# Attention denominators without the tensor engine: four one-column matmuls replaced, in 90 of 128 units, by a transposing VectorE sum and five GpSimd instructions

## The chip, the cores and the metric

The kernel runs on one core of a Trainium2 chip. Five engines with instruction queues of their own take part: TensorE (PE in the profile, its weight loads listed as PEld), VectorE (DVE), ScalarE (ACT), GpSimd (POOL) and SyncE (SP), which here only starts transfers. Engines meet through semaphores. The metric is the device time of one execution in microseconds (us); lower is better.

## The reference

The input `A_x` (2048 rows of 512) is normalised per row. Two branches start from the result `xn`, and their product is added to the input:

```
xn = layernorm(x)
s  = attention(xn, k_cache, v_cache, wq, wo)   # 32 heads of 128, 2048 queries, 2048 keys
g  = silu(mixer_mlp(xn, w1, w2, w3, w4))
return x + s * g
```

In the attention, `q = xn @ wq`, `p = softmax(q k^T / sqrt(128))`, `o = p v` for each head, and the heads' outputs are multiplied by `wo` and added. The softmax needs, for every query and head, the sum of 2048 exponentials; `o` is divided by it. Matrices are bfloat16; the scores need no maximum subtracted, since the inputs are small.

## The kernel before

The start (to about 147 us) computes layernorm, the mixer and most of the MLP. The attention follows and takes nearly all of the rest. It is cut into 128 units: 8 groups of 4 heads, in each group 4 blocks of 512 queries, in each block the 4 heads (`units`, head innermost). A unit is computed with keys on the partitions and queries along the free axis, in 8 slots (`SPU`), so that the main loop counts slots `n`, and `u, p = divmod(n, 8)`.

In slot p of unit u these things are issued, in this order:

- `s_slot(u, p)`: two matmuls of 128 keys by 512 queries into one PSUM tile `ps_s` (two buffers), and ScalarE's `exp` of it into a quarter of `pT` (L283).
- `pv_slot`, five slots behind: two matmuls that add `v` times those exponentials to `ps_o` (two buffers, each held from slot 5 of its unit until `norm` has read it).
- in slots 0 and 1 `q_mm(u + 1)`, two matmuls each, that make the next unit's queries in the one PSUM buffer tagged `xa`; in slot 2 VectorE's `q_copy` (L267) empties it.
- in slot 0 `add_last(u - 1)`: the exponentials of a unit are added up on VectorE over the 16 key blocks, with `add_first` (L289, slot 4), `add_next` (L294, slot 6 and slot 0 of the next unit) and two halving adds (L299, L300). What is left is `acc[:, 0, :]`: 128 partitions (keys) by 512 queries, still to be summed over the partitions.
- in slot 2 `norm(u - 2)` (L333): VectorE multiplies `ps_o` by the reciprocal denominators `rb` and writes `oT`.
- in slot 3 `sums(u - 1)` (L311 to L321): four matmuls with a quarter of `acc` each as the weights (every fourth query) and a column of ones as the moving side sum over the partitions, into 128x4 numbers in PSUM (also tag `xa`). VectorE's `reciprocal` (L319) reads them, and SP stores the result `rc` to a small DRAM tile `dr` (L321).
- in slot 4 `bcast(u - 1)` (L325): SP reads `dr` back, copied to all 128 partitions, as `rb`, 128 by 512 floats.
- in slots 4 to 6 `wo_mm` and `wo_post` for one finished 128-row tile of a block: four matmuls, and VectorE's add into `sacc` (L365).

All instructions are kept in the order of the program on their engine (`pin`). SP's queue therefore holds, per unit, the store of `rc`, the load of `rb` behind it, and behind these, in slots 5 to 7, the loads of the next group's keys (`load_k`, L132), values (`load_v`, L142) and weights. The keys of a group's last head are loaded in slots 5 and 7 of two successive units just ahead of the unit that uses them.

GpSimd's queue holds small layernorm work at the start (`rsqrt`, L167 an add and L168 a power, on 128x1 numbers) and the loads of `x` for the last group's outputs (`fin_load`, L355, emitted from unit 117 on); in the units between it has nothing.

Of the kernel before, what the change touches and what calls it, by code (L numbers as in the profile page):

```python
# [9 lines left out]
ALU = mybir.AluOpType  # L10
FP32 = mybir.dt.float32
# [6 lines left out]
def kernel(  # L18
# [15 lines left out]
    nc = tc.nc  # L34
    P = nc.NUM_PARTITIONS
# [15 lines left out]
    HG = 4  # L51
# [10 lines left out]
    pin = tc.keep_in_program_order  # L62

    def pool(name, bufs=1, space=None, **kw):
        if space is not None:
            kw["space"] = space
        return tc.tile_pool(name=name, bufs=bufs, **kw)

    ent = ctx.enter_context
    const = ent(pool("const"))  # L70
    xnT = const.tile([P, DC, Sq], BF16, name="xnT")
    xall = const.tile([P, NT, D], BF16, name="xall")
    ones_t = const.tile([P, 1], BF16, name="ones_t")
    nhalf = const.tile([P, 1], FP32, name="nhalf")
    mv1 = const.tile([P, NT, nc.vector.BN_AGGR_DIM], FP32, name="mv1")
    mv2 = const.tile([P, NT, nc.vector.BN_AGGR_DIM], FP32, name="mv2")
    rs1 = const.tile([P, NT], FP32, name="rs1")
# [9 lines left out]
    smp = ent(pool("smp", 4))  # L87
    tokp = ent(pool("tok", 4))
    drp = ent(pool("drp", 4, bass.MemoryType.DRAM))
# [15 lines left out]
    def mm(out, lhsT, rhs, start, stop):  # L105
        pin(nc.tensor.matmul(out=out, lhsT=lhsT, rhs=rhs, start=start, stop=stop))  # L106

    pin(nc.vector.memset(warm[:], 0.0))
    pin(nc.vector.memset(ones_t[:], 1.0))
    pin(nc.vector.memset(nhalf[:], -0.5))  # L110
    pin(nc.gpsimd.iota(diag[:], pattern=[[-1, P]], base=0, channel_multiplier=1,
                       allow_small_or_imprecise_dtypes=True))
    pin(nc.vector.tensor_scalar(
        out=ident[:], in0=diag[:], scalar1=0.0, scalar2=None, op0=ALU.is_equal))

    units = [(g, qt, hh) for g in range(NG) for qt in range(QT) for hh in range(HG)]
    NU = len(units)
    NS = NU * SPU
    kTs, vBs, wqs, wos, oTs, st = {}, {}, {}, {}, {}, {}
# [136 lines left out]
    def q_mm(u, dcs, tag="xa"):  # L256
        g, qt, hh = units[u]
        if dcs[0] == 0:
            st[u] = dict(psq=psX.tile([P, 512], FP32, tag=tag, name="ps_q"))
        for dc in dcs:  # L260
            mm(st[u]["psq"][:], wqs[g * HG + hh][:, dc, :],
               xnT[:, dc, qt * 512:(qt + 1) * 512], dc == 0, dc == DC - 1)

    def q_copy(u, eng=None):
        qT = qtp.tile([P, 512], BF16, name="qT")
        if eng is None:
            pin(nc.vector.tensor_copy(out=qT[:], in_=st[u].pop("psq")[:]))  # L267
        else:
            pin(nc.scalar.activation(out=qT[:], in_=st[u].pop("psq")[:], func=ACT.Identity))
        st[u]["qT"] = qT  # L270

    def s_slot(u, p):
        g, qt, hh = units[u]
        s = st[u]
        sps = psS.tile([P, 2, 512], FP32, name="ps_s")
        for j in range(2):
            kc = 2 * p + j
            kv = kTs[g * HG + hh].rearrange("d (i p j) -> d i j p", p=P, j=KJ)
            mm(sps[:, j, :], kv[:, kc // KJ, kc % KJ, :], s["qT"][:], True, True)
        if p % 2 == 0:  # L280
            s.setdefault("pT", []).append(pB.tile([P, 4, 512], BF16, tag="pT", bufs=4, name="pT"))
        jj = 2 * (p % 2)
        pin(nc.scalar.activation(  # L283
            out=s["pT"][-1][:, jj:jj + 2, :], in_=sps[:], func=ACT.Exp, scale=SCALE))
# [7 lines left out]
    def add_next(u, i):  # L292
        a = st[u]["acc"]
        pin(nc.vector.tensor_tensor(out=a[:], in0=a[:], in1=st[u]["pT"][i][:], op=ALU.add))  # L294

    def add_last(u):
        add_next(u, 3)
        a = st[u]["acc"]
        pin(nc.vector.tensor_tensor(out=a[:, 0:2, :], in0=a[:, 0:2, :], in1=a[:, 2:4, :], op=ALU.add))  # L299
        pin(nc.vector.tensor_tensor(out=a[:, 0, :], in0=a[:, 0, :], in1=a[:, 1, :], op=ALU.add))  # L300

    def pv_slot(u, p):
        g, qt, hh = units[u]
        s = st[u]
        if p == 0:
            s["o"] = psO.tile([P, 512], FP32, tag="ps_o", name="ps_o")
        pT = s["pT"][p // 2]
        for j in range(2):
            kc = 2 * p + j
            mm(s["o"][:], vBs[g * HG + hh][:, kc, :], pT[:, 2 * (p % 2) + j, :], kc == 0, kc == KC - 1)  # L310

    def sums(u):
        s = st[u]
        ps = psX.tile([P, 4], FP32, tag="xa", name="ps_sum")
        a = s["acc"][:, 0, :].rearrange("k (p j) -> k j p", j=4)
        for j in range(4):
            mm(ps[:, j:j + 1], a[:, j, :], ones_t[:], True, True)
        rc = smp.tile([P, 4], FP32, name="rc")
        pin(nc.vector.reciprocal(out=rc[:], in_=ps[:]))  # L319
        s["dr"] = drp.tile([P, 4], FP32, name="dr")  # L320
        pin(nc.sync.dma_start(out=s["dr"][:], in_=rc[:]))  # L321

    def bcast(u):
        st[u]["rb"] = pB.tile([P, 512], FP32, tag="rb", bufs=2, name="rb")
        pin(nc.sync.dma_start(  # L325
            out=st[u]["rb"][:], in_=st[u]["dr"][:].rearrange("p j -> (p j)").partition_broadcast(P)))

    def norm(u):
        g, qt, hh = units[u]
        s = st.pop(u)  # L330
        if hh == 0:
            oTs[(g, qt)] = pB.tile([P, HG, 512], BF16, tag="oT", bufs=2, name="oT")
        pin(nc.vector.tensor_tensor(  # L333
            out=oTs[(g, qt)][:, hh, :], in0=s["o"][:], in1=s["rb"][:], op=ALU.mult))
# [8 lines left out]
    def wo_mm(g, t, hhs, ps=None):  # L343
        if hhs[0] == 0:
            wo_box[0] = psX.tile([P, D], FP32, tag="xm", name="ps_wo") if ps is None else ps
        oT = oTs[(g, t // 4)]
        ts = t % 4
        for hh in hhs:
            mm(wo_box[0][:], oT[:, hh, ts * P:(ts + 1) * P], wos[g * HG + hh][:], hh == 0, hh == HG - 1)
# [3 lines left out]
    def fin_load(t):  # L353
        xl = tokp.tile([P, D], BF16, tag="ta", bufs=10, name="xl")
        pin(nc.gpsimd.dma_start(out=xl[:], in_=xsrc[t]))  # L355
        fin[t] = xl

    def wo_post(g, t):
        ps = wo_box.pop(0)
        if g == 0:  # L360
            sacc[t] = pS.tile([P, D], FP32, tag="sacc", bufs=NT, name="sacc")
            pin(nc.vector.tensor_copy(out=sacc[t][:], in_=ps[:]))
            return
        sa = sacc[t][:]
        pin(nc.vector.tensor_tensor(out=sa, in0=ps[:], in1=sa, op=ALU.add))  # L365
        if g < NG - 1:
            return
        xl, gl = fin.pop(t), xall[:, t, :]
        pin(nc.vector.scalar_tensor_tensor(  # L369
            out=gl, in0=sa, scalar=0.5, in1=gl, op0=ALU.mult, op1=ALU.mult))  # L370
        pin(nc.vector.tensor_tensor(out=xl[:], in0=gl, in1=xl[:], op=ALU.add))  # L371
        pin(nc.sync.dma_start(out=out2d[t * P:(t + 1) * P, :], in_=xl[:]))
# [158 lines left out]
            at(n + 4, lambda: gate_silu(t, th["a"]))  # L531

    wo_todo = deque()
    for n in range(NS + 3 * SPU):
        u, p = divmod(n, SPU)
        if u < NU:
            g, qt, hh = units[u]
            s_slot(u, p)
        m = n - LAG
        if 0 <= m < NS:  # L540
            pv_slot(*divmod(m, SPU))
        if p in (0, 1) and 4 * HG - 1 <= u < NU - 1:
            q_mm(u + 1, (2 * p, 2 * p + 1))
        if p == 0 and 1 <= u <= NU:
            add_last(u - 1)
        if p == 2 and 4 * HG - 1 <= u < NU - 1:
            q_copy(u + 1)
        if p == 2 and 2 <= u <= NU + 1:
            norm(u - 2)
            if units[u - 2][2] == HG - 1:  # L550
                gg, qq = units[u - 2][:2]
                wo_todo.extend((gg, 4 * qq + ts) for ts in range(4))
                if gg == NG - 1:
                    fin_load(4 * qq)
        if p == 3 and 1 <= u <= NU:
            sums(u - 1)
        if p == 4 and 1 <= u <= NU:
            bcast(u - 1)
        if p in (4, 5) and wo_todo:
            wo_mm(*wo_todo[0], (0, 1) if p == 4 else (2, 3))  # L560
        if p == 6 and wo_todo:
            gg, t = wo_todo.popleft()
            wo_post(gg, t)
            if gg == NG - 1 and t % 4 < 3:
                fin_load(t + 1)
        if p == 4 and u < NU:
            add_first(u)
        if p == 6 and u < NU:
            add_next(u, 2)
        held_mm(n)  # L570
        for fn in todo.pop(n, ()):
            fn()
        if not held and not todo.get(n + 1) and pS is None and n >= 4 * SPU + 5:
            right.close()
            pS = right.enter_context(pool("pS", side="right", reuse_waits="tile"))
# [38 lines left out]
```

## Time and profile before

| what | value |
|---|---|
| median of 3 runs | 1289.25 us (1289.19 to 1290.49) |
| the profiled execution | 1289.44 us, its span 1287.6 us, so 1.84 us lie around the span |
| granted TensorE clock, mean | 0.991 |
| PE busy | 1257.4 us, 98% of the span |
| ACT busy | 1054.8 us, 82% |
| DVE busy | 942.5 us, 73% |
| POOL busy | 47.5 us, 4%, nearly all of it before 76 us and after 1175 us |
| `norm` of unit to `norm` of unit, 330 to 1110 us | 89 of them from 334.8 to 1106.5: 8.77 us each |

The span is the time from the first to the last instruction. A group line gives busy time, then the mean duration of one, then how long its engine sat idle just before and who ended that. Overlapping matmuls are drawn longer than they keep the engine from the next, so distances between starts tell more than durations.

### The profile page before, as it was taken

What the parts mean: (1) busy time and instruction counts of PE and PEld (TensorE: products, weight loads), DVE (VectorE), ACT (ScalarE), POOL (GpSimd) and SP (SyncE); (2) the same over time, 40 slices, a digit from 0 to 9 for tenths busy, and PEclk for the clock granted to TensorE, in tenths of its full rate; (3) what the DMA queues carried; (4) which work ended last, traced back from release to release, by engine and by line L of the source; (5) the groups of instructions that cost most, each with busy time, mean ns of one, the idle gap of its engine ahead of it and who ended that gap; (6) DMA issues with size and microseconds to landing.
All of it is one profiled execution on the core that took longest, in us unless ns stands there. A gap on an engine that the chain in (4) does not pass through costs nothing.

```text
span 1287.6 us, 16764 instructions
## 1 busy us (share of the span) xinstructions
PE 1257.4 (98%) x6128; PEld 609.6 (47%) x6252; DVE 942.5 (73%) x1316; ACT 1054.8 (82%) x1101; POOL 47.5 (4%) x115
## 2 busy tenths in 40 slices
PE   7999999999999999999999999999999999999995
PEld 3444444444444444444444444444444444444442
DVE  6721467777777777777777777777777777778886
ACT  4344779998888888888888888888888888888882
POOL 5320000000000000000000000000000000000000
PEclk9999999999999999999999999999999999999997
DMA  9293122443144522452145423451244323442211
GB/s 209 45 172 74 21 46 50 82 91 67 41 74 77 97 34 51 90 96 46 48 83 77 79 42 59 90 95 33 55 91 78 62 51 72 85 82 43 65 43 49
DMA packets 170771, 91.57 MB, mean 71 GB/s; under 512 B 124928, under 2 KB 153088, under 8 KB 170688
## 3 DMA queue, kind: packets, MB, share of 16 engines
q1 hardware_dynamic: 166464, 84.72, 34.3%
q0 software_dynamic: 1824, 4.98, 1.7%
q8 instruction: 49, 0.80, 0.3%
q10 hardware_dynamic: 2400, 0.79, 0.2%
q14 instruction: 34, 0.28, 0.1%
HBM read 67.63 MB, written 2.36 MB: 54 GB/s over the span
## 4 chain that ended last, share of the span: by engine, by line
PE 89%; DVE 6%; DMA 2%; ACT 1%; issue 1%; POOL 0%; another core or an unknown queue 0%; SPq 0%; DVEq 0%; ACTq 0%
PE ps_s L106 36%; PE ps_o L106 35%; PE ps_wo L106 8%; PE ps_q L106 7%; DVE acc L294 2%; PE ps_m L106 2%; PE ps_sum L106 1%; ACT pT L283 1%; DVE sacc L365 1%; DVE xall L369 1%; DVE acc L299 1%; DMA kT<-in_A_k_cache_dram 1%; DVE qT L267 0%; DVE xl L371 0%; DMA xnT<-xall 0%
## 5 line engine op out<-in xcount | busy, mean ns | idle before, releaser
L283 ACT ACTIVATE pT<-ps_s 128x1024 bf16<-128x1024 f32 x1024 | 993.1, 1026 | 135.3 <-PE ps_s L106 130.4
L106 PE MATMUL ps_o<-pT,vb 128*128 128x512 bf16 x2030 | 605.0, 379 | 3.3
L106 PE MATMUL ps_s<-qT,kT 128*128 128x512 bf16 x1986 | 596.8, 380 | 3.9 <-ACT pT L283 1.2
L294 DVE TENSOR_TENSOR acc<-acc,pT 128x2048 bf16<-128x2048 bf16 x256 | 312.3, 1220 | 72.3 <-ACT pT L283 71.2
L106 PEld LDWEIGHTS <-kT 128*128 128x128 bf16 x2048 | 222.0, 113 | 203.0 <-issue 6.1
L106 PEld LDWEIGHTS <-vb 128*128 128x128 bf16 x2048 | 199.9, 98 | 225.7
L289 DVE TENSOR_TENSOR acc<-pT 128x2048 bf16<-128x2048 bf16 x128 | 156.8, 1225 | 51.2 <-ACT pT L283 51.2
L106 PE MATMUL ps_wo<-wo_h,oT 128*128 128x512 bf16 x509 | 154.5, 387 | 6.2 <-DVE sacc L365 3.1
L365 DVE TENSOR_TENSOR sacc<-ps_wo,sacc 128x512 f32<-128x512 f32 x112 | 77.4, 691 | 89.5 <-PE ps_wo L106 88.7
L106 PE MATMUL ps_q<-xnT,wq_h 128*128 128x512 bf16 x481 | 141.6, 379 | 0.2
L299 DVE TENSOR_TENSOR acc<-acc 128x1024 bf16<-128x1024 bf16 x128 | 88.5, 691 | 4.4
L333 DVE TENSOR_TENSOR oT<-ps_o,rb 128x512 bf16<-128x512 f32 x128 | 87.3, 682 | 2.6 <-DMA rb<-dr 2.6
L106 PEld LDWEIGHTS <-oT 128*128 128x128 bf16 x512 | 50.4, 99 | 70.2 <-issue 7.6
L106 PEld LDWEIGHTS <-wq_h 128*128 128x128 bf16 x512 | 50.0, 98 | 60.4 <-issue 0.3
L267 DVE CAST qT<-ps_q 128x512 bf16<-128x512 f32 x112 | 76.3, 682 | 0.0
L300 DVE TENSOR_TENSOR acc<-acc 128x512 bf16<-128x512 bf16 x128 | 54.4, 425 | 4.4
L106 PEld LDWEIGHTS <-acc 128*128 128x128 bf16 x512 | 37.6, 116 | 34.2 <-issue 4.0
L355 POOL DMA_DIRECT2D xl<-in_A_x_dram x16 | 8.7, 543 | 1137.4 <-DMA out_dram<-xl 1014.3
L106 PE MATMUL ps_s<-xn2T,w_sb 128*128 128x512 bf16 x220 | 48.6, 379 | 0.2
L106 PEld LDWEIGHTS <-w_sb 128*128 128x128 bf16 x304 | 30.0, 99 | 39.1 <-issue 7.7
L234 ACT ACTIVATE h2T<-ps_s 128x1024 bf16<-128x1024 f32 x28 | 28.7, 1024 | 24.0 <-PE ps_s L106 23.3
L319 DVE RECIPROCAL rc<-ps_sum 128x4 f32<-128x4 f32 x128 | 23.2, 181 | 21.3 <-PE ps_sum L106 7.2
(45 smaller groups left out, 332.2 us busy)
## 6 DMA issues: line engine op xcount, KB each, us to landing
rb<-dr SPq DMA_DIRECT2D x128, 256.0 KB, 4.3
vb<-in_A_v_cache_dram SPq DMA_DIRECT2D x64, 256.0 KB, 4.4
wo_h<-in_A_wo_dram SPq DMA_DIRECT2D x32, 128.0 KB, 4.2
wq_h<-in_A_wq_dram SPq DMA_DIRECT2D x28, 128.0 KB, 4.5
w_sb<-in_B_w_dram SPq DMA_DIRECT2D x9, 256.0 KB, 5.4
kT<-in_A_k_cache_dram SPq DMA_TRANSPOSE x128, 4.4
xl<-in_A_x_dram POOLq DMA_DIRECT2D x16, 128.0 KB, 2.3
dr<-rc SPq DMA_DIRECT2D x128, 2.0 KB, 1.4
```

Of the source, the lines that this page charges most:

```text
L106: pin(nc.tensor.matmul(out=out, lhsT=lhsT, rhs=rhs, start=start, stop=stop))
L234: pin(nc.scalar.activation(out=h2[c, f][:], in_=ps[:], func=ACT.Gelu_apprx_tanh))
L267: pin(nc.vector.tensor_copy(out=qT[:], in_=st[u].pop("psq")[:]))
L283: pin(nc.scalar.activation(out=s["pT"][-1][:, jj:jj + 2, :], in_=sps[:], func=ACT.Exp, scale=SCALE))
L289: pin(nc.vector.tensor_tensor(out=s["acc"][:], in0=s["pT"][0][:], in1=s["pT"][1][:], op=ALU.add))
L294: pin(nc.vector.tensor_tensor(out=a[:], in0=a[:], in1=st[u]["pT"][i][:], op=ALU.add))
L299: pin(nc.vector.tensor_tensor(out=a[:, 0:2, :], in0=a[:, 0:2, :], in1=a[:, 2:4, :], op=ALU.add))
L300: pin(nc.vector.tensor_tensor(out=a[:, 0, :], in0=a[:, 0, :], in1=a[:, 1, :], op=ALU.add))
L319: pin(nc.vector.reciprocal(out=rc[:], in_=ps[:]))
L333: pin(nc.vector.tensor_tensor(out=oTs[(g, qt)][:, hh, :], in0=s["o"][:], in1=s["rb"][:], op=ALU.mult))
L365: pin(nc.vector.tensor_tensor(out=sa, in0=ps[:], in1=sa, op=ALU.add))
L369: pin(nc.vector.scalar_tensor_tensor(out=gl, in0=sa, scalar=0.5, in1=gl, op0=ALU.mult, op1=ALU.mult))
```

## The change

For the units 20 to 109 (`TURN`, 90 of 128) the sum over the partitions and the reciprocal are made in another way, and issued in slot 1 instead of slot 3:

1. VectorE reads `acc[:, 0, :]` in one `tensor_reduce` with 32x32 transposition. The 512 queries are seen as 32 by 16 with a step of 16 elements along the summed axis; each block of 32 partitions is transposed against 32 queries and added up, which gives `pr`, 128x16 floats: for each of the four blocks of 32 keys, 32 partitions by 16 partial sums.
2. GpSimd adds the four blocks: it copies the upper 64 partitions down to a tile of their own and adds them, then does the same with partitions 32 to 63, so that 32x16 sums are left.
3. GpSimd raises them to the power -1 (against a constant tile `mone`, one more memset at the start).
4. SP stores 32x16 floats to `dr`, in 32 rows of 64 bytes where there were 128 rows of 16. `bcast` is unchanged.

The other 38 units keep the old function under the name `sums_pe`, in slot 3.

```diff
-    def sums(u):
+    def sums_pe(u):
         s = st[u]
         ps = psX.tile([P, 4], FP32, tag="xa", name="ps_sum")
...
-        s["dr"] = drp.tile([P, 4], FP32, name="dr")
+        s["dr"] = drp.tile([P, 4], FP32, name="dr4")
         pin(nc.sync.dma_start(out=s["dr"][:], in_=rc[:]))
 
+    def sums(u):
+        s = st[u]
+        a = s["acc"][:, 0, :].rearrange("k (i c) -> k c i", c=16)
+        pr = smp.tile([P, 16], FP32, name="pr")
+        pin(nc.vector.tensor_reduce(
+            out=pr[:], in_=a, axis=mybir.AxisListType.X, op=ALU.add, apply_transpose=True))
+        for w in (64, 32):
+            up = smp.tile([w, 16], FP32, name=f"up{w}")
+            pin(nc.gpsimd.tensor_copy(out=up[:], in_=pr[w:2 * w, :]))
+            pin(nc.gpsimd.tensor_tensor(out=pr[0:w, :], in0=pr[0:w, :], in1=up[:], op=ALU.add))
+        rc = smp.tile([32, 16], FP32, name="rct")
+        pin(nc.gpsimd.tensor_tensor(out=rc[:], in0=pr[0:32, :], in1=mone[0:32, :], op=ALU.pow))
+        s["dr"] = drp.tile([32, 16], FP32, name="dr")
+        pin(nc.sync.dma_start(out=s["dr"][:], in_=rc[:]))
...
+    TURN = range(5 * HG, NU - 4 * HG - 2)
...
+        if p == 1 and u - 1 in TURN:
+            sums(u - 1)
...
-        if p == 3 and 1 <= u <= NU:
-            sums(u - 1)
+        if p == 3 and 1 <= u <= NU and u - 1 not in TURN:
+            sums_pe(u - 1)
```

More of the change, by code (lines that the diff above doesn't have):

```diff
@@ L74 @@
     nhalf = const.tile([P, 1], FP32, name="nhalf")
+    mone = const.tile([P, 16], FP32, name="mone")
     mv1 = const.tile([P, NT, nc.vector.BN_AGGR_DIM], FP32, name="mv1")
@@ L110 @@
     pin(nc.vector.memset(nhalf[:], -0.5))
+    pin(nc.vector.memset(mone[:], -1.0))
     pin(nc.gpsimd.iota(diag[:], pattern=[[-1, P]], base=0, channel_multiplier=1,
```

## The prediction

> **What bounds the kernel now.** First I read the page's chain of waits by line, then its groups, then the timeline of one unit, and last the chain around the odd entries of the first list.
>
> ```profile
> PE 89%; DVE 6%; DMA 2%; ACT 1%; issue 1%; POOL 0%; another core or an unknown queue 0%; SPq 0%; DVEq 0%; ACTq 0%
> PE ps_s L106 36%; PE ps_o L106 35%; PE ps_wo L106 8%; PE ps_q L106 7%; DVE acc L294 2%; PE ps_m L106 2%; PE ps_sum L106 1%; ACT pT L283 1%; DVE sacc L365 1%; DVE xall L369 1%; DVE acc L299 1%; DMA kT<-in_A_k_cache_dram 1%; DVE qT L267 0%; DVE xl L371 0%; DMA xnT<-xall 0%
> ...
> L294 DVE TENSOR_TENSOR acc<-acc,pT 128x2048 bf16<-128x2048 bf16 x256 | 312.3, 1220 | 72.3 <-ACT pT L283 71.2
> L106 PE MATMUL ps_sum<-ones_t,acc 128*128 128x1 bf16 x512 | 34.5, 172 | 4.0 <-DVE acc L300 2.5 <-DVE qT L267 1.6
> L168 POOL TENSOR_TENSOR rs<-ve,nhalf 128x1 f32<-128x1 f32 x32 | 18.3, 572 | 2.7
> ```
>
> TensorE is the limit: 89% of the chain, and in the steady units nobody keeps it waiting. The matmuls to be removed are drawn at 34.5 us, but pipelined durations overlap, so their price comes from distances in the timeline of a unit:
>
> ```profile
> 605.86 0.42 DVE L300 TENSOR_TENSOR acc<-acc 128x512 bf16<-128x512 bf16 x1
> 606.21 0.68 DVE L267 CAST qT<-ps_q 128x512 bf16<-128x512 f32 x1
> 606.81 0.68 DVE L333 TENSOR_TENSOR oT<-ps_o,rb 128x512 bf16<-128x512 f32 x1
> 607.32 0.27 PE L106 MATMUL ps_sum<-ones_t,acc 128*128 128x1 bf16 x4
> 607.45 0.60 PE L106 MATMUL ps_s<-qT,kT 128*128 128x512 bf16 x2
> 607.63 0.18 DVE L319 RECIPROCAL rc<-ps_sum 128x4 f32<-128x4 f32 x1
> 607.84 0.32 SPq L321 DMA_DIRECT2D dr<-rc  x1
> 608.26 1.23 DVE L289 TENSOR_TENSOR acc<-pT 128x2048 bf16<-128x2048 bf16 x1 [0.45 <-ACT pT L283]
> 609.18 0.60 PE L106 MATMUL ps_o<-pT,vb 128*128 128x512 bf16 x2
> 609.27 0.32 SPq L325 DMA_DIRECT2D rb<-dr  x1
> 611.77 0.60 PE L106 MATMUL ps_s<-qT,kT 128*128 128x512 bf16 x2
> 615.57 0.68 DVE L333 TENSOR_TENSOR oT<-ps_o,rb 128x512 bf16<-128x512 f32 x1
> 616.22 0.60 PE L106 MATMUL ps_s<-qT,kT 128*128 128x512 bf16 x2
> ```
>
> Slots 4 to 7 hold 20 large matmuls and nothing else: 607.45 to 611.77, 4.32 us. Slots 0 to 3 hold 20 and the four small ones: 611.77 to 616.22, 4.45 us. The four cost 0.13 us.
>
> The chain by line has a K load on it, 1%, which a TensorE-bound kernel should not. Followed to its place:
>
> ```profile
> 441.04 1.58 DMA dr<-rc
> 442.63 0.32 SPq L325
> 443.00 6.58 DMA kT<-in_A_k_cache_dram
> 449.62 0.62 PE ps_s L106 x2
> ```
>
> The keys of a group's last head are queued on SP behind the store and reload of the denominators, and here TensorE met them late, by about 0.16 us (this score matmul is 0.33 us behind the small ones that start at 449.29; at 607.32 the distance is 0.13).
>
> **The change part by part.**
>
> *Removed from TensorE:* four loads and matmuls, 0.13 us, in 90 units: 11.7 us. Nothing is next in line to take it. ScalarE's exponentials need 8 x 1.03 = 8.2 us of a unit that goes from 8.77 to 8.64, and slots 2 and 3 become what 6 and 7 are, where TensorE waits for nothing.
>
> *The VectorE sum.* 512 bf16 elements in, few out; no row has its transposition. The nearest is the statistics row, also 512 bf16 into a few floats, 0.68 us; a plain bf16 pass of 512 took 0.42. I take 0.68, with 0.42 and 1.23 (three 0.41 us passes; the add of four times the elements) as ends. Page rule: the Trainium skill's "SBUF — State Buffer", section "Door 1: The DMA port swizzle", says that reads which touch each 16-byte line only once pay a penalty; this read steps 32 bytes. The trace has 116 against 98 ns for weights read with an 8-byte step, and no wider step. An estimate by that rule, at half rate, is 1.2 us, which the upper end already holds and which leaves the sum as it is.
>
> Who waits for the sum: it stands before the query copy and `norm` on VectorE, and moves both by 0.68 us. The copy ends near 607.6 and is needed at 611.77. `norm` ends at 608.17 instead of 607.49 and frees the PSUM tile for the matmul at 609.18 (609.05 now): 0.88 us left, and 0.33 at 1.23. The first add (L289) can start 0.82 us after `norm` starts, at about 608.38 instead of 608.26; the 0.76 us that VectorE idles ahead of L365 takes that. The reciprocal's 0.18 us goes. VectorE's three waits in a unit, 0.45 + 0.76 + 0.58 = 1.79 us, shrink by 0.68 - 0.18 and by the 0.13 shorter unit to 1.16. So it costs 0.
>
> *The GpSimd chain.* The layernorm rows start an add 0.09 us after VectorE's result and a second instruction 0.31 us after the first. Two copies and two adds of 16 columns: 4 x 0.31 = 1.24 us (the iota over 128 columns took only 0.24, so columns as such are cheap). The power took 0.57 us for one column, 0.35 more than the 0.22 add. For 16 columns the ends are 0.57 (all of it fixed) and 0.57 + 15 x 0.35 = 5.8 (none of it). I take 1.0, a guess of 0.03 us for each further column: nearer the only power row, because loops on this engine stream cheaply in the iota row.
>
> So `rc` is ready at 606.96 + 0.09 + 1.24 + 1.0 = 609.29 instead of 607.81, 1.48 us later although issued two slots earlier. Store and reload as before (dr issue to rb issue 1.43, rb landing 4.3): `rb` lands at about 615.05, and `norm` asks for it at 615.57 + 0.68 - 0.13 = 616.12. 1.07 us to spare: 0. The store's 32 pieces instead of 128 I price at 0, between 1.4 less and 1.3 more (it landed in 1.4 to 2.7 us in the steady units).
>
> *SP's queue.* Its wait for `rc` now ends 1.48 us later, and the reload and the key loads behind it move too. In the five group changes within `TURN` the third quarter of the last head's keys was issued at 443.0, 583.3, 723.6, 863.9 and 1004.1 and landed 6.6, 5.1, 5.2, 5.2 and 5.5 us later. TensorE wanted it at about 449.4, 589.9, 730.3, 870.4 and 1010.7 (0.39 us before the `dr` issue of that unit): to spare -0.2, 1.5, 1.5, 1.4 and 1.1. A shift of 1.48 makes the first 1.5 us later than it was, the last about 0.4 late and the others just on time: 2 us. Ends: 1 us with a power of 0.57, 6 us if VectorE's sum takes 1.23 too; more only in the rivals.
>
> *GpSimd's queue.* The first ten loads of `x` that ran by 190 us now queue behind unit 109's chain. They are wanted from unit 117 on, some 60 us later: 0. The memset: 0.06 us at the start, hidden by input loads.
>
> **Sum:** 1289.44 - 11.7 + 2.0 = 1279.7 us, against the profiled execution, which lies 0.2 us above the median shown.
>
> **Rivals.**
>
> *GpSimd and VectorE block each other; slower.* The chain's four small steps end about 1.33 us after the sum and the first add comes about 1.42 after it, so the power is in flight when a VectorE add with two memory inputs wants to start. The trace has one kind of blocking:
>
> ```profile
> 7.78 0.41 DVE L177 TENSOR_SCALAR xall<-xin,mv,rs 128x512 bf16<-128x512 bf16 x1
> ```
>
> ```profile
> 7.92 0.35 POOL L167 TENSOR_SCALAR ve<-mv 128x1 f32<-128x1 f32 x1 [0.18 <-DVE mv L173]
> 8.35 0.57 POOL L168 TENSOR_TENSOR rs<-ve,nhalf 128x1 f32<-128x1 f32 x1
> ```
>
> Alone this GpSimd add took 0.22; beside VectorE it took 0.35 and ended 0.08 us after VectorE's instruction. If the power holds the add likewise, VectorE has 1.16 us of idle time to give; each unit then lengthens by what is beyond, and at a hold of 1.29 us the gain is gone (about 1.2 with the K loads). A power of 2 us gives (2.0 - 1.29) x 90 = 64 us more than before, 1353; one of 5.8 some 400 more. For it: the arithmetic per column, 0.35 us at worst. Against: no two-input add overlaps GpSimd arithmetic in this trace. The Trainium skill ("SBUF — State Buffer", section "Who interferes with whom") says that a VectorE instruction with two SBUF inputs and a GpSimd one that reads SBUF exclude each other, whoever starts first; by it the threshold above applies. The row just shown agrees for another kind of VectorE instruction.
>
> *Only the latency counts; slower.* Nothing blocks, but the power is long. `norm` may run 1.55 us later than now (609.05 - 607.49) before TensorE waits for its PSUM tile, so the chain may last 4.27 us after the sum, the power 2.9. Beyond, a unit lengthens by about half of the excess, since the loop sum, reload, `norm`, next sum closes over two units; the K loads slip too. Power 4 us: 0.55 x 90 = 50, less 11.7, plus 5 x 3: about 1343.
>
> *Gain eaten, no change.* A sum of 1.23 and a power near 1.2 put late keys (6 us) and a few VectorE waits of 0.06 us a unit (5 us) against the 11.7: about 1289.
>
> *It does not do what it says:* TensorE's gap filled by another wait at once. Slots 4 to 7 speak against it; no chance of its own.
>
> **How the numbers follow.** Forecast, power up to about 1.2 us or no blocking and up to some 2.5: 0.53, with a range of its own of 1276 to 1286. Gain eaten: 0.07. Blocking: 0.25. Latency: 0.15. A measurement here tells 0.2%, 2.6 us, from no change. Faster 0.53, same 0.07, slower 0.40. The slower cases spread from 1292 upward with their middle near 1345; leaving out their upper half, the range is 1275.5 to 1345.
>
> **What the profile would show.** Right: no `ps_sum` in the steady units, `norm` to `norm` 8.64 us; a reduction of about 0.68 us between L300 and the query copy; the power starting about 1.3 us after it and lasting about 1; `rb` issued about 1.5 us later; no VectorE wait for `rb`; short TensorE waits for keys at the group changes. Wrong: L289 or L294 waiting for or stretched beside GpSimd, `norm` waiting for `rb`, TensorE waiting for `norm`, a unit above 8.77 us. The power's duration decides.

## The result and the profile after

| | before | after |
|---|---|---|
| median (range) of 4 runs | 1289.42 us (1289.19 to 1290.49) | 1305.38 us (1303.57 to 1307.44) |
| profiled execution, its span | 1289.44 us, 1287.6 us | 1307.44 us, 1305.6 us |
| GpSimd busy | 47.5 us | 426.5 us |
| `norm` to `norm` inside the changed units | 8.77 us | 8.95 us (86 units from 353.34 to 1123.42) |

The changed kernel is slower: the ratio of times is 1.0118, with a 95% interval of 1.0106 to 1.0130. The forecast was 1279.7 us; the time lies inside the range of 1275.5 to 1345, and on the other side of no change.

The page of after, the chain by engine and by line, and two groups (busy time, mean ns, idle time before):

```profile
PE 52%; DVE 15%; DMA 14%; POOL 12%; ACT 5%; issue 2%; SPq 0%; DVEq 0%; POOLq 0%; ACTq 0%
PE ps_s L107 21%; PE ps_o L107 19%; POOL rct L336 9%; DMA rb<-dr 7%; PE ps_wo L107 6%; DVE acc L296 5%; ACT pT L285 4%; DMA dr<-rct 3%; PE ps_q L107 3%; DVE pr L329 2%; DMA kT<-in_A_k_cache_dram 2%; DVE acc L301 2%; PE ps_m L107 2%; DVE oT L350 2%; DVE acc L302 1%
...
L336 POOL TENSOR_TENSOR rct<-pr,mone 32x16 f32<-32x16 f32 x90 | 306.8, 3409 | 7.0
L329 DVE TRANSPOSE_TENSOR_REDUCE pr<-acc 128x16 f32<-128x512 bf16 x90 | 100.1, 1112 | 9.0
```

TensorE's share of the chain fell from 89% to 52%. The denominators' path stands in its place: GpSimd's power, the store and reload, the sum. The power is drawn at 3.41 us in the mean, where I had taken 1.0, and VectorE's sum at 1.11, where I had taken 0.68. `ps_sum` is gone from the changed units.

A mean of 3.41 hides two values. The timeline of after shows two units in a row (start, length, engine and line):

```profile
611.74 0.69 DVE L350 TENSOR_TENSOR oT<-ps_o,rb 128x512 bf16<-128x512 f32 x1 [0.23 <-DMA rb<-dr]
...
612.11 2.90 POOL L336 TENSOR_TENSOR rct<-pr,mone 32x16 f32<-32x16 f32 x1
612.35 1.22 DVE L291 TENSOR_TENSOR acc<-pT 128x2048 bf16<-128x2048 bf16 x1
...
620.10 0.69 DVE L350 TENSOR_TENSOR oT<-ps_o,rb 128x512 bf16<-128x512 f32 x1
620.49 0.21 POOL L334 TENSOR_TENSOR pr<-pr,up 32x16 f32<-32x16 f32 x1
620.70 1.22 DVE L291 TENSOR_TENSOR acc<-pT 128x2048 bf16<-128x2048 bf16 x1
620.78 3.90 POOL L336 TENSOR_TENSOR rct<-pr,mone 32x16 f32<-32x16 f32 x1
...
629.39 0.69 DVE L350 TENSOR_TENSOR oT<-ps_o,rb 128x512 bf16<-128x512 f32 x1 [0.54 <-DMA rb<-dr]
629.46 2.90 POOL L336 TENSOR_TENSOR rct<-pr,mone 32x16 f32<-32x16 f32 x1
630.00 1.22 DVE L291 TENSOR_TENSOR acc<-pT 128x2048 bf16<-128x2048 bf16 x1
```

The power takes 2.90 us when the add L291 starts after it (0.24 and 0.54 us here), and 3.90 when the add is already running (by 0.08 us). So it is in all 90 changed units: 44 powers are short, with the add 0.24 to 2.02 us behind their start, and 46 are long, with the add 0.07 to 0.17 us ahead. Short and long alternate, with one exception. `norm` (L350) stands 8.36 us behind the one before (611.74 to 620.10) and then 9.29 us (to 629.39). The chain of waits, followed through the long one (start, length, what):

```profile
620.78 3.91 POOL rct L336
624.70 1.32 DMA dr<-rct
626.04 0.04 issue
626.08 3.29 DMA rb<-dr
629.39 0.70 DVE oT L350
630.10 0.04 issue
630.14 0.59 PE ps_o L107 x2
...
638.40 3.91 POOL rct L336
```

This is the new limit read from top to bottom: power, store, reload, `norm`, and TensorE standing until `norm` frees its PSUM tile. Two units later the chain is at a power again, a long one, 17.62 us behind the first; two units of 8.67 us, as the experiments below have them without a slow power, would take 17.34. The waits of after (us in total, times, longest) say how much of it TensorE feels:

```profile
DVE oT L350 <- DMA rb<-dr: 36.8, 47, 3.5
PE ps_o L107 <- DVE oT L350: 13.1, 20, 1.8
PE ps_s L107 <- DMA kT<-in_A_k_cache_dram: 7.2, 5, 1.7
```

In before, `norm` waited 2.6 us in all for `rb`. From start to start of TensorE's matmuls, which counts what a matmul's drawn length hides, the delays ahead of `ps_o` add up to about 20 us, and the five at the group changes, where keys come late, are 0.68, 1.84, 1.80, 1.90 and 1.84, about 8 us. Together that is 28 us, as much as after's profiled execution lies above the forecast (1307.44 - 1279.7 = 27.7).

### The profile page after: what moved, and what is told of

It reads as the page before. It is cut to its first block, busy times and chain, and to the rows that moved or that the text cites. A ratio compares the mean times of both kernels' runs of the same rounds, so it can differ in the third digit from the quotient of the medians.

```text
span 1305.6 us, 16734 instructions
## 1 busy us (share of the span) xinstructions
PE 1261.7 (97%) x5892; PEld 597.8 (46%) x5892; DVE 1018.4 (78%) x1317; ACT 1055.4 (81%) x1101; POOL 426.5 (33%) x565
## 4 chain that ended last, share of the span: by engine, by line
PE 52%; DVE 15%; DMA 14%; POOL 12%; ACT 5%; issue 2%; SPq 0%; DVEq 0%; POOLq 0%; ACTq 0%
PE ps_s L107 21%; PE ps_o L107 19%; POOL rct L336 9%; DMA rb<-dr 7%; PE ps_wo L107 6%; DVE acc L296 5%; ACT pT L285 4%; DMA dr<-rct 3%; PE ps_q L107 3%; DVE pr L329 2%; DMA kT<-in_A_k_cache_dram 2%; DVE acc L301 2%; PE ps_m L107 2%; DVE oT L350 2%; DVE acc L302 1%
## 5 line engine op out<-in xcount | busy, mean ns | idle before, releaser
L107 PE MATMUL ps_o<-pT,vb 128*128 128x512 bf16 x2048 | 608.2, 379 | 14.1 <-DVE oT L350 13.1
L107 PE MATMUL ps_s<-qT,kT 128*128 128x512 bf16 x2048 | 609.1, 379 | 8.5 <-DMA kT<-in_A_k_cache_dram 7.2
L296 DVE TENSOR_TENSOR acc<-acc,pT 128x2048 bf16<-128x2048 bf16 x256 | 312.5, 1221 | 72.4 <-ACT pT L285 71.2
L107 PEld LDWEIGHTS <-kT 128*128 128x128 bf16 x2048 | 229.3, 114 | 234.2 <-DMA kT<-in_A_k_cache_dram 10.1
L336 POOL TENSOR_TENSOR rct<-pr,mone 32x16 f32<-32x16 f32 x90 | 306.8, 3409 | 7.0
L333 POOL COPY up<-pr 64x16 f32<-64x16 f32 (+1 forms) x180 | 34.1, 189 | 651.1 <-DVE pr L329 645.4
L291 DVE TENSOR_TENSOR acc<-pT 128x2048 bf16<-128x2048 bf16 x128 | 155.8, 1217 | 10.0 <-ACT pT L285 10.0
L107 PE MATMUL ps_q<-xnT,wq_h 128*128 128x512 bf16 x512 | 147.8, 379 | 0.0
L350 DVE TENSOR_TENSOR oT<-ps_o,rb 128x512 bf16<-128x512 f32 x128 | 87.7, 685 | 36.8 <-DMA rb<-dr 36.8
L329 DVE TRANSPOSE_TENSOR_REDUCE pr<-acc 128x16 f32<-128x512 bf16 x90 | 100.1, 1112 | 9.0
L269 DVE CAST qT<-ps_q 128x512 bf16<-128x512 f32 x112 | 73.4, 655 | 0.0
```

The costliest lines, as they stand in the source:

```text
L291: pin(nc.vector.tensor_tensor(out=s["acc"][:], in0=s["pT"][0][:], in1=s["pT"][1][:], op=ALU.add))
L329: pin(nc.vector.tensor_reduce(out=pr[:], in_=a, axis=mybir.AxisListType.X, op=ALU.add, apply_transpose=True))
L333: pin(nc.gpsimd.tensor_copy(out=up[:], in_=pr[w:2 * w, :]))
L336: pin(nc.gpsimd.tensor_tensor(out=rc[:], in0=pr[0:32, :], in1=mone[0:32, :], op=ALU.pow))
L350: pin(nc.vector.tensor_tensor(out=oTs[(g, qt)][:, hh, :], in0=s["o"][:], in1=s["rb"][:], op=ALU.mult))
```

## The experiments

In the expectations P is the theory that the power is the cost, by its length and by what that makes late; D is its rival, that the rest of the change is: the VectorE sum, the query copy and `norm` moved behind it. Later C stands for the collision of power and add, L for the power's own length. Ratios are to the kernel before, with 95% intervals; times are medians.

### The power, or the rest of the change

**e1_mult** puts a multiplication where the power was:

```diff
-        pin(nc.gpsimd.tensor_tensor(out=rc[:], in0=pr[0:32, :], in1=mone[0:32, :], op=ALU.pow))
+        pin(nc.gpsimd.tensor_tensor(out=rc[:], in0=pr[0:32, :], in1=mone[0:32, :], op=ALU.mult))
```

> The changed kernel with its power replaced by a multiplication of the same 32x16 numbers, so that the denominators are used without being inverted; all else stays. Theory P (the power's 2.9 to 3.9 us make rb late: norm waits, TensorE waits for norm's PSUM tile, and the K loads behind the store slip): rc comes about 1.0 us later than before the change instead of 3.7 to 4.7, TensorE no longer waits for norm, late keys cost 1 to 2 us, 1279 us. Rival D (the 1.11 us VectorE sum ahead of the query copy and norm is what delays TensorE): TensorE's waits for norm, some 13 to 20 us, stay: 1295 to 1305 us.

Measured: 1280.09 us, ratio 0.9917 (0.9902 to 0.9931). The whole loss is gone, and the removed matmuls show their gain: P holds and D falls. The timeline and the group of e1_mult show one thing more:

```profile
613.59 1.22 DVE L291 TENSOR_TENSOR acc<-pT 128x2048 bf16<-128x2048 bf16 x1
613.67 1.21 POOL L336 TENSOR_TENSOR rct<-pr,mone 32x16 f32<-32x16 f32 x1
```

```profile
L336 POOL TENSOR_TENSOR rct<-pr,mone 32x16 f32<-32x16 f32 x90 | 108.6, 1207 | 7.0
```

The GpSimd add of the same 32x16 numbers one step earlier takes 0.21 us (L334 above). The multiplication is drawn at 1.21 us in the mean of all 90 units, and in every one it ends 0.07 to 0.08 us after VectorE's add. In the one unit where it starts 0.18 us behind the add's start and not 0.08 it is that much shorter, 1.11. So about 1.0 us of it is waiting for that add, and the 1.0 us between the two lengths of the power is the same wait.

**e2_dve_recip** leaves the sum and the small steps and gives the inversion back to VectorE, in slot 3 behind `norm`. It computes the full result:

```diff
-        pin(nc.gpsimd.tensor_tensor(out=rc[:], in0=pr[0:32, :], in1=mone[0:32, :], op=ALU.pow))
+        s["pr"] = pr
+    def recip(u):
+        s = st[u]
...
+        pin(nc.vector.reciprocal(out=rc[:], in_=s["pr"][0:32, :]))
...
+        if p == 3 and u - 1 in TURN:
+            recip(u - 1)
```

> The changed kernel with VectorE's reciprocal (32x16, slot 3, behind norm) in place of GpSimd's power. P: rc about 1.0 us later than before the change, VectorE waits at most 0.1 us a unit for GpSimd's last add: 1279 to 1280 us, 10 us faster than the kernel before. D: 1295 us or more, as for the multiplication.

Measured: 1280.11 us, ratio 0.9915 (0.9901 to 0.9930). This version beats both kernels. The chain by engine on its page, and the reciprocal among its groups of instructions:

```profile
PE 89%; DVE 6%; ACT 1%; issue 1%; DMA 1%; POOL 1%; another core or an unknown queue 0%; DVEq 0%; SPq 0%; ACTq 0%
```

```profile
L340 DVE RECIPROCAL rct<-pr 32x16 f32<-32x16 f32 x90 | 21.7, 241 | 0.0
```

TensorE is back at the 89% of before. 0.24 us on VectorE do what took GpSimd 2.90 to 3.90. Against e2_dve_recip, the `norm` of the same unit in after falls behind by 1.1 us at the 25th unit, 8.4 at the 61st, 17.7 at the 85th and 27.8 at the 115th, and no further: the loss builds up through the changed units and nowhere else.

### What the matmuls were worth, and what the VectorE sum costs

**e4_no_matmuls** is the kernel before without the four small matmuls in the 90 units:

```diff
-        ps = psX.tile([P, 4], FP32, tag="xa", name="ps_sum")
+        if skip:
+            ps = s["acc"][:, 0, 0:4]
+        else:
+            ps = psX.tile([P, 4], FP32, tag="xa", name="ps_sum")
```

> The kernel before with the four one-column matmuls left out in the 90 units; the reciprocal reads 128x4 elements of acc instead, so that the sum over the partitions is missing. The price of the removed work by itself. Both theories: 90 x 0.13 = 11.7 us less, 1277.7 us. If the gap is filled by another wait: nearer to 1289.

Measured: 1280.56 us, ratio 0.9919 (0.9905 to 0.9934). Its units take 8.67 us and not 8.64, so the matmuls were worth 0.10 us in each unit; expected were 0.13 and 1277.7 us. In e4_no_matmuls and in e2_dve_recip alike, 19 of a unit's 20 pairs of large matmuls follow each other by 0.43 us and one by 0.47; in before none does. I take this one for the score matmul of slot 4 that now meets ScalarE's exponential of slot 2 a little early: in all 88 units looked at it starts 0.05 us after an exponential ends. That is argued from its place, and no run isolated it.

**e3_extra_sum** adds the VectorE sum, unused, to the kernel before:

```diff
+        if p == 1 and u - 1 in TURN:
+            pr = smp.tile([P, 16], FP32, name="pr")
+            pin(nc.vector.tensor_reduce(
+                out=pr[:], in_=st[u - 1]["acc"][:, 0, :].rearrange("k (i c) -> k c i", c=16),
+                axis=mybir.AxisListType.X, op=ALU.add, apply_transpose=True))
```

> The kernel before with one part of the change alone: the VectorE sum with transposition is added in slot 1 of the same 90 units, its result unused; the four matmuls stay. P: its 1.11 us go into VectorE's 1.79 us of waiting, 1289 to 1291 us. D: norm and what follows come late for TensorE, 1300 us or more.

Measured: 1357.55 us, ratio 1.0514 (1.0497 to 1.0532). The expectation missed by 67 us, and the waits of e3_extra_sum say why:

```profile
PE ps_sum L106 <- DVE qT L267: 54.1, 99, 0.6
```

In before this line has 1.6 us. The four matmuls and the next unit's queries share the PSUM buffer `xa`. With the sum in front of it the query copy empties that buffer too late for matmuls that are still there, and TensorE stands 0.75 us ahead of them in each unit. The experiment put together two things that the change never has at once, so it cannot speak of D. **e10_sum_no_matmuls** takes them apart: the edits of e3_extra_sum and e4_no_matmuls together.

> The run without the four matmuls (the sum over the partitions is missing there) with the VectorE sum added in slot 1, its result unused. If the extra sum cost 67 us beside the matmuls only because these wait for the PSUM buffer that the delayed query copy empties: 1280 us, the same as without it. If it delays TensorE through norm or the adds: 1290 us or more.

Measured: 1280.29 us, ratio 0.9933 (0.9921 to 0.9946), like e4_no_matmuls. Without the matmuls the sum's 1.11 us on VectorE costs nothing, as the prediction had argued.

### The key loads

**e5_k_early** issues the keys in slot 0, ahead of the denominators' store and reload on SP's queue:

```diff
-                at((b - 2 + (2 * hh + i // 2 + (hh > 0))) * SPU + (5, 7)[i % 2], lambda h=h, i=i: load_k(h, (i,)))
+                at((b - 2 + (2 * hh + i // 2 + (hh > 0))) * SPU, lambda h=h, i=i: load_k(h, (i,)))
```

> The changed kernel with the key loads issued in slot 0 of their units instead of slots 5 and 7, so that they stand ahead of the unit's store and reload on SP's queue. P with its second term: TensorE's five waits for keys (8 us in the profile after) go, the waits for norm stay: about 1297 us. If the late keys come from contention and not from the queue's order: 1305 us.

Measured: 1304.98 us, ratio 1.0119 (1.0104 to 1.0134), the same as after. TensorE's waits for keys are gone. In the waits of e5_k_early another has grown, from 13.1 us in 20 places:

```profile
PE ps_o L107 <- DVE oT L350: 16.9, 34, 0.9
```

From start to start these delays are 24.5 us, where they were 20, so about half of the 8 us has come back there. The other half is the distance of the two profiled executions (1303.87 and 1307.44), the lowest and the highest of their four; the medians differ by 0.4. Late keys and late denominators draw on the same slack: a unit that stands for its keys gives the next `rb` time to arrive. The 8 us were really spent in after, but they were not there to be won alone. **e8_recip_k_early** does the same to e2_dve_recip.

> VectorE's reciprocal in place of the power, and the key loads issued in slot 0. P with its second term: nothing is late, the whole 11.7 us are gained: 1277 to 1278 us, better than both kernels. D: 1290 us or more.

Measured: 1279.88 us, ratio 0.9927 (0.9910 to 0.9944), some 2 us above what was expected and no change against 1280.11: with the reciprocal on VectorE the keys are in time anyway.

### The length of the power

**e6_two_powers** runs a second power, unused, ahead of the first:

```diff
+        r2 = smp.tile([32, 16], FP32, name="r2")
+        pin(nc.gpsimd.tensor_tensor(out=r2[:], in0=pr[0:32, :], in1=mone[0:32, :], op=ALU.pow))
```

> The changed kernel with a second, unused power of the same size ahead of the first, 2.9 us more in the chain. P: the chain sum, power, store, reload, norm closes over two units, so each unit lengthens by about half of it, 1.45 us: 90 x 1.45 = 130, about 1435 us. D: GpSimd's time does not matter, about 1306 us. Mutual blocking (a VectorE add waits while a power runs): up to 2.9 us a unit, about 1560 us.

Measured: 1477.8 us, ratio 1.1460 (1.1426 to 1.1494). The time follows the power, by about 1.9 us a unit for 2.9 us more of it. Half of the excess, as my latency rival had it, would be 1.45. The profiled execution shows where the rest lies, from start to start of TensorE's matmuls. Against after, the delays ahead of `ps_o` grew by some 111 us (20 to 132), which is 1.2 us a unit and a little less than the half; those for keys grew by 13 (8 to 21). A further 42 us are 201 matmuls that follow the one before by about twice the usual 0.216 us. All of them lie in 26 stretches, 102 us in all, in which the granted TensorE clock was 0.5; in the changed units of after it was 1.0 throughout. Each of these stretches comes with a stand of TensorE of 2.4 to 4.8 us for `norm` or for keys; not every such stand brings one. So a quarter of the excess is a slower TensorE and not the chain. A GpSimd that held VectorE for its whole length would have given some 1560.

**e7_half_power** raises 8 of the 16 columns and leaves the others as ones:

```diff
-        rc = smp.tile([32, 16], FP32, name="rct")
-        pin(nc.gpsimd.tensor_tensor(out=rc[:], in0=pr[0:32, :], in1=mone[0:32, :], op=ALU.pow))
+        rc = rcc[u % 4]
+        pin(nc.gpsimd.tensor_tensor(
+            out=rc[:, 0:8], in0=pr[0:32, 0:8], in1=mone[0:32, 0:8], op=ALU.pow))
```

> The changed kernel with the power on 8 of the 16 columns; the other 8 columns of rc are ones, so half of the denominators are left out. If the power costs 0.57 us for the first column and 0.155 for each further (2.9 for 16), it takes 1.65 us, or 2.65 where VectorE's add starts first. P: rc is then at the edge of what norm can bear, late keys cost some 5 us: 1280 to 1287 us. D: 1295 to 1306 us.

Measured: 1285.06 us, ratio 0.9962 (0.9947 to 0.9977), as expected. The power is drawn at 1.64 us at its shortest and at 2.63 in nearly all units, again 1.0 apart. With the layernorm's one column (0.57, on 128 partitions and with exponent -0.5) and the full 16 (2.90) this makes a straight line: (1.64 - 0.57) / 7 = 0.15 and (2.90 - 0.57) / 15 = 0.155 us for each further column.

### Why long and short alternate

C says: the wait behind the add is what decides whether `rb` is late, and a late `norm` pushes the add of the next unit behind the power, so that every second unit escapes. Then an add that is always a little later would stop the waits. L says that the power's own 2.9 us is enough. **e9_add_behind_power** puts a useless VectorE instruction between `norm` and the add:

```diff
+        if p == 3 and u - 1 in TURN:
+            gap = smp.tile([32, 16], FP32, name="gap")
+            pin(nc.vector.reciprocal(out=gap[:], in_=mone[0:32, :]))
```

> The changed kernel with one useless VectorE instruction of 0.24 us (a 32x16 reciprocal) behind norm, so that the add L291 starts about 0.16 us after the power instead of 0.08 us before it. Theory C (the power of 2.9 us by itself just fits; what makes rb late is the 1.0 us that GpSimd waits whenever the add started first): every power takes 2.9, the alternation ends, norm never waits: 1280 to 1285 us, although VectorE has more to do. Rival L (2.9 us is too long by itself): units stay at 8.8 us on average, 1300 us or more. Rival V (an add that comes second waits for the whole power): VectorE loses up to 2.9 us a unit, 1350 us or more.

**e12_gap_two** and **e13_gap_three** hold that reciprocal two and three times.

> As the run with one useless VectorE reciprocal behind norm, but with two (0.46 us): the add L291 then starts about 0.3 us after the power's drawn start, not 0.08. C (the 1.0 us that GpSimd waits beside the add is the loss): powers of 2.9 throughout, rb lands some 0.4 us before norm asks for it, 1280 to 1286 us, although VectorE works 41 us more than in the changed kernel. L (2.9 us is too long by itself): still 1300 us or more, with norm waiting for rb in units whose power took 2.9.

> The same with three (0.69 us), the add about 0.5 us behind the power's start. C: as with two if that distance sufficed, 1280 to 1288 us; if two are still too near, this one shows the change. L: 1300 us or more. If VectorE itself becomes the limit (its idle time in a unit falls to about 0.1 us): units of 8.8 us or more with no wait for rb.

Measured: 1307.2, 1310.76 and 1312.17 us, ratios 1.0131 (1.0106 to 1.0155), 1.0168 (1.0129 to 1.0208) and 1.0181 (1.0158 to 1.0205). The alternation stayed, with 2.90 against 3.99 us in e9_add_behind_power and about 4.1 and 4.2 in the others. In the long cases the filler is itself running when the power starts (in e9_add_behind_power from 0.09 us before to 0.14 behind), and the power ends 2.76 us after the add's end, as the long ones of after do. In e13_gap_three it does so although the add starts 0.3 us behind the power's start, and in after a distance of 0.24 us was enough for a short power. I read this as GpSimd waiting for the filler as well as for the add. These three decide nothing between C and L. **e14_gap_stats** uses a filler of another kind, statistics over a constant tile:

```diff
+        if p == 3 and u - 1 in TURN:
+            gap = smp.tile([P, nc.vector.BN_STATS_DIM], FP32, name="gap")
+            pin(nc.vector.bn_stats(out=gap[:], in_=warm[:, 0:256]))
```

> The gap of reciprocals took part in the blocking itself: with it the power still ended 2.76 us after the add's end although it was drawn as starting up to 0.3 us before the add. Here the useless VectorE instruction behind norm is a statistics pass over 256 elements (about 0.4 us), a kind beside which GpSimd's add and power kept their 0.22 and 0.57 us at the start of the kernel. The add L291 comes about 0.3 us after the power's start. C (the 1.0 us wait beside the add is the loss): powers of 2.9 throughout, no wait for rb, 1280 to 1286 us. L (2.9 us is too long by itself): 1300 us or more.

Measured: 1291.72 us (10 runs), ratio 1.0013 (1.0003 to 1.0023). Useless work on VectorE made the changed kernel some 14 us faster. Its timeline, then its power's group on the page, then its waits:

```profile
626.05 2.90 POOL L336 TENSOR_TENSOR rct<-pr,mone 32x16 f32<-32x16 f32 x1
626.31 1.21 DVE L291 TENSOR_TENSOR acc<-pT 128x2048 bf16<-128x2048 bf16 x1
```

```profile
L336 POOL TENSOR_TENSOR rct<-pr,mone 32x16 f32<-32x16 f32 x90 | 261.0, 2900 | 7.1
```

```profile
DVE oT L350 <- DMA rb<-dr: 11.7, 14, 2.9
```

Every power now takes 2.90 us, with the add 0.17 us or more behind its start (0.26 here), and `norm` waits 14 times and not 47. **e15_gap_stats_long** doubles the filler's elements to 512.

> The same with 512 elements (0.68 us), the add about 0.6 us after the power's start. C: 1280 to 1290 us, the upper end if VectorE is then nearly full. L: 1300 us or more.

Measured: 1293.2 us, ratio 1.0019 (1.0008 to 1.0030): as much, so the place of the add matters and not the filler's length.

Of the 25 us between after (1305.4) and the same kernel without a power (1280.1), about 14 are the collision, C. The other 11 or 12 stay with every power at 2.90: that is L, and neither theory's number was met. In the profiled execution of e14_gap_stats, the fastest of its ten, TensorE's delays are 5.6 us for keys, at the five group changes, and 3.0 us ahead of `ps_o`, in 8 places. Together they are 8.6 of the 9.7 us by which it lies above that of e2_dve_recip (1289.65 and 1279.99). In that execution L is for the larger part late keys, the term that the prediction had at 2 us; no run issued the keys earlier beside this filler.

### The store in larger pieces

After's reloads and loads land about 1 us sooner than before's, which the prediction had priced at nothing. **e11_no_matmuls_64b** is e4_no_matmuls with the reciprocals stored as 32 rows of 64 bytes:

```diff
-        rc = smp.tile([P, 4], FP32, name="rc")
+        rs = [32, 16] if skip else [P, 4]
+        rc = smp.tile(rs, FP32, name=f"rc{rs[0]}")
...
-        s["dr"] = drp.tile([P, 4], FP32, name="dr")
+        s["dr"] = drp.tile(rs, FP32, name=f"dr{rs[0]}")
```

> The run without the four matmuls, with the reciprocal of 32x16 elements and the store in 32 rows of 64 bytes instead of 128 of 16 (the sum over the partitions is missing in both). If the size of the stored pieces is what makes the transfers of the changed kernel land 1 us sooner: rb 3.3 us and keys 3.5 us to landing instead of 4.4 and 4.7. If it is the timing of GpSimd's chain: 4.3 and 4.6 as before. The time is the same in both, 1280 us.

Measured: 1279.65 us, ratio 0.9923 (0.9910 to 0.9936), no change of time against e4_no_matmuls. The DMA issues (KB each, median us from issue to landing) of e4_no_matmuls and of e11_no_matmuls_64b, over all 128 units:

```profile
rb<-dr SPq DMA_DIRECT2D x128, 256.0 KB, 4.3
```

```profile
rb<-dr SPq DMA_DIRECT2D x128, 256.0 KB, 3.3
```

The pieces of the store alone make the reload land 1 us sooner, and the keys behind it too (4.6 to 3.5 us).

## Why the prediction was wrong

*The step that failed* is the power: "I take 1.0, a guess of 0.03 us for each further column". Measured are 0.155 us a column and 2.90 us in all. The bounds of 0.57 and 5.8 held it; the choice between them did not. I leaned on the iota over 128 columns, a cheap instruction of another kind, although the only row of a power stood at 0.35 us above the add for one column. The power grows by 0.155 us with every column, where the GpSimd add took 0.22 us for one column and 0.21 for 16; 2.90 lies near the middle of the two ends, 3.2.

*The second failing term* is a wait that is missing from the sum: the power also stands about 1.0 us behind VectorE's two-input add. The blocking rival had these two meeting at the right place and the wrong way round: it let the power hold VectorE. The prediction put the add 0.09 us behind the power's start (1.42 against 1.33 us after the sum); by the prediction's own steps, `norm` at 607.49 and the add 0.82 later, that is 608.31 and not 608.38, so 0.02 us. Which of the two comes first was open, and in after it changes from unit to unit.

In after that add is never stretched: L291 keeps its 1.22 us (mean 1217 ns, 1225 for the same add in before), also when it starts 0.24 us into a power of 2.90, and it is GpSimd that waits. Only in e6_two_powers is an add stretched: where a power starts 0 to 0.06 us ahead of the add on line L296, one of the two waits, the add by up to 0.07 us or the power by 1.1. With the power 0.08 us or more ahead the add takes its usual time.

The Trainium skill ("SBUF — State Buffer", section "Who interferes with whom") says that such a pair excludes each other; e1_mult agrees for GpSimd, with 1.0 us. As the rival had used it, with the power holding the add to its end, the add at 626.31 in e14_gap_stats would have waited until 628.95. It did not, and the measurement decides.

*What happened is the latency rival*, which I gave 0.15: the chain ends too late for `norm`, TensorE waits for `norm`'s PSUM tile, the keys slip behind it on SP's queue. Its threshold was a power of 2.9 us. The reload lands 1.0 us sooner (e11_no_matmuls_64b), the sum takes 0.43 longer and the small steps 0.16 less (1.17 us from the sum's end to the power's start, 1.33 predicted), so the threshold moves to about 2.9 + 1.0 - 0.43 + 0.16 = 3.6 us. Short powers stay below it and long ones exceed it, which is why only every second unit pays, and why its 1343 us for 4 us of power was too much. Three of the four signs that the prediction had named for being wrong are in the profile (`norm` waiting for `rb`, TensorE for `norm`, units above 8.77 us); the fourth, the blocking rival's own, a VectorE add that waits or is stretched beside GpSimd, is not.

*The other steps.* The removed matmuls: 11.7 us predicted, 9 to 10 measured (e4_no_matmuls), because 0.03 us of a unit went to a wait that follows. The VectorE sum: mis-sized, 1.11 for 0.68 and inside its ends; its cost of 0 was right (e10_sum_no_matmuls). The Trainium skill ("SBUF — State Buffer", section "Door 1: The DMA port swizzle") names a penalty for reads that touch each 16-byte line only once, and gives no size. The half rate in my estimate of 1.2 us was my own; 1.11 lies near it, and no run shows whether the step of the read is the reason. The key loads: right in mechanism, 8 us for the 2 forecast. Counted from the end of the halving adds, `rc` was ready after 0.10 + 1.11 + 1.17 + 2.90 or 3.90 = 5.3 or 6.3 us, where it had taken 1.53 (606.28 to 607.81): 3.8 to 4.8 us later and not 1.5. With some 1.4 us to spare and landings 1.0 sooner that is 1.4 to 2.4 us late, and 1.84 was measured. But it was not a term to add (e5_k_early). The store's pieces: priced at 0, and worth 1 us of latency.

Had the power cost what I took, the forecast would have stood: with a short instruction in its place e1_mult and e2_dve_recip gave 1280.1 us, against 1279.7 on record. That they agree to 0.4 us is partly luck: the matmuls were priced about 2 us too high, and the 2 us for late keys were not lost there (e8_recip_k_early).

## What to carry to other kernels

Before a function moves to another engine, price it from a row of that same function there, for each column, and let its whole latency run through the loop that it closes, not only its engine's idle share: GpSimd was busy for a third of the span and still set the pace. Look at which instruction of the neighbour runs at the moment when the moved one starts; a shift of about a third of a microsecond decided 1.0 us here. When a group's mean length lies between two values that alternate from unit to unit, look for a loop in which being late cures itself for one round.

## What the runs showed of the hardware

- A GpSimd multiplication of 32x16 numbers that finds VectorE's two-input add running is drawn 1.21 us and ends with it (e1_mult), where an add of as many took 0.21. The other way round there was next to no wait: the add starts 0.24 us or more into a power of 2.90 and takes its usual 1.22 (after). Where a power started 0 to 0.06 us ahead of an add, the add took up to 0.07 us longer (e6_two_powers).
- GpSimd's power: 0.57 us for one column (before), 1.64 for 8 (e7_half_power), 2.90 for 16 (after); VectorE's reciprocal of the same 32x16 numbers 0.24.
- VectorE's sum with 32x32 transposition over 128x512 bf16: 1.11 us.
- 2 KB stored in 128 pieces of 16 bytes made the reload behind it land in 4.3 us, in 32 pieces of 64 bytes in 3.3.
- In the run with two powers the granted TensorE clock was 0.5 in 26 stretches, 102 us in all, each beside a stand of TensorE of 2.4 to 4.8 us; there 201 matmuls came about 0.43 us apart and not 0.216 (e6_two_powers).
- A useless instruction of 0.42 us on VectorE in each of 90 units made a kernel 14 us faster (e14_gap_stats).
